# Softmax sums' reciprocals spread over partitions and multiplied onto the product with v

## The chip, the cores and the metric

One core of a Trainium2 chip runs the whole program. The metric is the device time of one execution in microseconds (us), as the median of several runs. The engines are PE (TensorE: matmuls and transposes), ACT (ScalarE), DVE (VectorE), POOL (GpSimd) and SP (SyncE, which here only issues DMAs, in order, from one queue). SBUF is the on-chip memory, PSUM the memory that PE writes its sums to, and DRAM the chip's large memory.

## The reference

Attention with a block mask, then two feed-forward layers. The part that the change touches is the softmax, whose rows are divided by their sum before the product with v.

```
q, k, v: (4, 8, 576, 64)                       # batch, heads, sequence, head size
scores = q @ k.T / sqrt(64), masked where block_i < block_j (blocks of 64)
attn = exp(scores - max)
attn = attn / (sum(attn, axis=-1) + 1e-9)
x = (attn @ v) as (2304, 512)
h = x @ w_in (512 x 2048);   y = (max(h, 0) + log1p(exp(-|h|))) @ w_out (2048 x 512)
h = y @ u1 (512 x 1024);     s = h * softmax(h)
out = ((s - mean) / sqrt(var + 1e-6) * g_ln) @ u2 (1024 x 512)
```

## The kernel before

All work is cut into tasks (`add(engine, model ns, rank, function, dependencies)`). A planner (`Plan.run`) plays the tasks through with model durations, takes on each engine the ready task of lowest rank, and so fixes the order of the instructions of every engine; each engine then works through its list strictly in that order. The rank of a task is its local rank plus the numbers of two tables, `OFF` (by task) and `RANK` (by group).

Float32 values are split into a high and a low part (`..._hi`, `..._lo`, on paper x = hi + lo) so that PE can multiply them in a faster form with three matmuls (hi·hi, hi·lo, lo·hi). The groups are:

- **Piece**: one of 32 pieces of the weights w1 and w2 (512 KB each, 16 of each). `load` brings `raw` by DMA, `signed` (ACT) and `bits0`, `bits1` (DVE) turn it into a float32 `a`, `do_hi` (ACT or DVE) and `do_lo` (DVE) make the two parts of `w`.
- **UnitA**: two heads of one batch, the first 256 positions; 16 units, four to a chunk of 256 tokens (chunks 0 to 3). Tasks: `mm_qk` (PE), `mask`, two `max`, `scale` (DVE), `exp` (ACT, which also adds up the sums `dA`), `den0`, `den1` (DVE: sum + 1e-9, reciprocal), `norm` (DVE: four multiplications of `eA` by its rows' reciprocals), `tr` (PE transposes of `eA`), `copy` (to `psA`, ACT or DVE), `pv` (PE: product with v), `x_hi`, `x_lo` (to `xt`, the input of the first layer). Scores, transposes and product share a PSUM bank named `R`, `r`, `acc` or `hp`.
- **UnitC**: two heads of one batch, the other 320 positions; 16 units, for chunks 4 to 8. The 320 rows are worked on in three parts i = 0, 1, 2, with score matmuls S of 384, 512 and 288 columns; I write S(0), S(1), S(2). Per part: `mm_qk`, `mask`, `max`, `exp` (to `eC`, sums `dC`), `den0`, `den1`, `norm` (five multiplications a unit, ACT or DVE), `split` (16-bit halves to `hl`), `tr` (a DMA transpose back into `eC`, issued by SP), `merge` (DVE, to `ps`). Then `pv` (PE, to `O`), `x_hi`, `x_lo`.
- **Pair**: two of the 16 blocks of w1/w2 for one chunk. `a` (24 matmuls of 256 columns, `hp<-xt,w`), `abs`, `exp`, `ln` (ACT), `stt`, `do_gh`, `do_gl` (DVE), `b` (24 matmuls, `acc<-gh/gl,w`, for chunk 1 `R<-...`). 8 pairs a chunk, 72 in all. The list `SEQ` sets the order of the `a` parts: chunk 0 leads chunk 1 by LAG pairs, and each `a` waits for the one before it in `SEQ`; from chunk 2 on the chunks follow each other. The first `a` of a chunk needs the whole `xt` of that chunk.
- **Tok**: 18 blocks of 128 tokens through the second layer (`h<-...`, then `op<-...`).

The stages overlap: units of chunks 0 and 1 with the conversion of the weights (0 to about 53 us), then the pairs of chunks 0 and 1 with the rest of the conversion, UnitA of chunks 2 and 3, UnitC among the pairs (about 200 to 465 us), the last pairs, and Tok to the end.

Of the kernel before, what the change touches and what calls it, by code (L numbers as in the profile page):

```python
# [24 lines left out]
    "Pair.evac": -5005.0, "Pair.exp": -16485.4, "Pair.ln": -8885.4, "Pair.store": -7128.0, "Pair.stt": 8391.0,
    "Piece.bits0": 1146.4, "Piece.bits0@P0": -7429.7, "Piece.bits1": -9495.3, "Piece.bits1@P0": 8715.1,
    "Piece.do_hi": 9838.9, "Piece.do_hi@P0": 3547.5, "Piece.do_hi_g": 507.8, "Piece.do_lo": 6538.2,
    "Piece.do_lo@P": -11296.2, "Piece.do_lo@P0": -11338.9, "Piece.do_lo_g": 6022.5, "Piece.load": 13705.4,
    "Piece.load@P0": 16755.6, "Piece.signed": 15163.0, "Piece.signed@P0": -783.6, "Tok.a": 1079.7,
    "Tok.aggr": -16861.9, "Tok.bm": 10531.9, "Tok.center": -6983.1, "Tok.exp": 7716.2, "Tok.ln_hi": 9220.6,  # L30
    "Tok.ln_lo": 2618.6, "Tok.load": -16248.9, "Tok.logexp": -10340.8, "Tok.max": -5855.7, "Tok.merge": -13609.8,
    "Tok.mul": -11643.0, "Tok.o_evac": 12110.8, "Tok.small1": 12073.6, "Tok.small2": -5198.1, "Tok.split": -1245.7,
    "Tok.split_hi": 598.2, "Tok.split_lo": -8460.0, "Tok.stats": -9589.2, "Tok.store": 34066.3, "Tok.tr": -8072.5,
# [189 lines left out]
def body(ctx: ExitStack, tc: tile.TileContext, qk, qkA, vP, vA, w1, w2, u1, u2, gln, out):  # L223
# [126 lines left out]
    class UnitC:  # L350
# [96 lines left out]
        def max(self, i):  # L447
            self.m, self.den = self.t([128, 2], "mC", 3), self.t([128, 2], "dC", 3)
            n = 2 if i < 2 else 1
            DVE.tensor_reduce(out=self.m[:, 0:n], in_=self.scores(i), axis=AX.X if i < 2 else AX.XY, op=ALU.max, negate=True)  # L450
            self.stat = getattr(self, "stat", {})
            self.stat[i] = (self.m, self.den, n)

        def exp(self, i, j):
            m, den, _ = self.stat[i]
            e, sc = state["eC"][i][:, j, :], self.scores(i)
# [4 lines left out]
            ACT.activation(e, sc, AF.Exp, bias=m[:, j:j + 1], accum_out=den[:, j:j + 1])  # L461

        def den0(self, i):
            _, den, n = self.stat[i]
            DVE.tensor_scalar_add(den[:, 0:n], den[:, 0:n], 1e-9)

        def den1(self, i):
            _, den, n = self.stat[i]
            DVE.reciprocal(den[:, 0:n], den[:, 0:n])

        def norm(self, i, j, e):
            p, r = state["eC"][i][:, j, 0:WC[i]], self.stat[i][1][:, j:j + 1]
            if e == "ACT":
                ACT.activation(p, p, AF.Copy, scale=r)
            else:
                DVE.tensor_scalar(p, p, r, None, op0=ALU.mult)  # L476
# [601 lines left out]
```

## Time and profile before

| | us |
|---|---|
| median of 3 runs (760.71 to 765.06) | 762.73 |
| the profiled execution's own time | 761.89 |
| its span, first to last instruction | 760.1 |
| PE busy | 736.1 (97%) |
| DVE busy | 592.5 (78%) |
| ACT busy | 442.3 (58%) |

Matmuls are pipelined: a matmul's duration in the trace is longer than the distance to the next one, so runs of equal matmuls are read by the length of the run divided by their count. Line numbers (L606) are those of the kernel before; L232 is the helper that issues every matmul and L238/L240 the helper `copy` on ACT and on DVE.

### The profile page before, as it was taken

The page shows a single profiled execution, that of the slowest core. Times are in us where ns is not written, and L with a number is a line of the kernel's source. Part 1 is how long each engine was busy: PE and PEld are TensorE (multiplying, and loading weights), DVE is VectorE, ACT ScalarE, POOL GpSimd, SP SyncE. Part 2 cuts the span into 40 slices and gives each one's busy share as a digit, 9 for nine tenths or more (in the row PEclk, how much of TensorE's full clock was granted, in tenths as well). Part 3 has the DMA queues.
Part 4 walks back from the last instruction along what each step waited for, and adds up shares of the span by engine and source line. Part 5 has one row for each costly group of instructions (what it writes and reads, how often), then busy time and mean ns, then how long its engine had stood idle before and what let it go on. Part 6 is the DMA issues. An engine that isn't in the chain of part 4 may idle for free.

```text
span 760.1 us, 13785 instructions
## 1 busy us (share of the span) xinstructions
PE 736.1 (97%) x5304; PEld 650.0 (86%) x5304; DVE 592.5 (78%) x1273; ACT 442.3 (58%) x914; POOL 0.7 (0%) x6
## 2 busy tenths in 40 slices
PE   7678999999999999999999999999999999999998
PEld 4568999989988888888888889999998888888887
DVE  6999984476777888788889685656978998898882
ACT  6758774474877777877777772653923433333331
POOL 0000000000000000000000000000000000000000
PEclk9889999999999999999999999999999999999999
DMA  6665720121566556665556644325414554344322
GB/s 214 210 226 184 238 87 22 61 63 45 93 138 129 111 117 178 126 130 136 116 112 129 137 98 106 103 93 190 130 42 97 124 98 101 95 95 84 83 63 77
DMA packets 148002, 88.99 MB, mean 117 GB/s; under 512 B 119648, under 2 KB 131168, under 8 KB 147936
## 3 DMA queue, kind: packets, MB, share of 16 engines
q1 hardware_dynamic: 147936, 88.10, 46.6%
q8 instruction: 42, 0.69, 0.4%
q14 instruction: 24, 0.20, 0.1%
HBM read 49.29 MB, written 9.44 MB: 77 GB/s over the span
## 4 chain that ended last, share of the span: by engine, by line
PE 79%; DMA 8%; DVE 8%; ACT 3%; issue 1%; SPq 0%; ACTq 0%; DVEq 0%
PE hp L232 21%; PE acc L232 19%; PE op L232 13%; PE h L232 13%; DMA eC<-hl 6%; PE S L232 4%; PE R L232 4%; PE O L232 3%; PE r L232 2%; ACT eC L461 1%; DMA raw<-in_w_dram 1%; DVE ps L498 1%; DVE mC L450 1%; PE r L613 1%; DVE t L698 1%
## 5 line engine op out<-in xcount | busy, mean ns | idle before, releaser
L232 PE MATMUL hp<-xt,w 128*128 128x256 f32 x1728 | 219.7, 282 | 3.1 <-DVE t L698 1.9
L232 PEld LDWEIGHTS hp<-xt,w 128*128 128x128 f32 x1728 | 207.5, 190 | 13.8 <-issue 9.7
L232 PE MATMUL acc<-gh,w 128*128 128x256 f32 x768 | 146.1, 283 | 0.6 <-DVE gh L240 0.6
L232 PEld LDWEIGHTS acc<-gh,w 128*128 128x128 f32 x768 | 122.9, 191 | 3.8 <-issue 1.6
L232 PE MATMUL acc<-gl,w 128*128 128x256 f32 x384 | 108.0, 281 | 0.3 <-DVE gl L706 0.3
L232 PE MATMUL h<-u,w 128*128 128x512 f32 x432 | 100.7, 389 | 0.0
L232 PE MATMUL op<-w,w2w 128*128 128x512 f32 (+1 forms) x456 | 100.5, 378 | 0.0
L232 PEld LDWEIGHTS op<-w,w2w 128*128 128x128 f32 x456 | 82.5, 188 | 16.0
L232 PEld LDWEIGHTS h<-u,w 128*128 128x128 f32 x432 | 80.8, 188 | 16.5
L232 PEld LDWEIGHTS acc<-gl,w 128*128 128x128 f32 x384 | 73.1, 190 | 0.7 <-DVE gl L706 0.6
L689 ACT ACTIVATE t<-hp 128x512 f32<-128x512 f32 x72 | 42.7, 594 | 46.9 <-PE hp L232 40.5
L698 DVE SCALAR_TENSOR_TENSOR t<-hp,t 128x512 f32<-128x512 f32 x72 | 49.3, 684 | 18.6 <-ACT t L695 18.3
L498 DVE COPY ps<-eC 128x1536 uint16<-128x1536 uint16 (+2 forms) x48 | 45.8, 954 | 21.2 <-DMA eC<-hl 21.2
L461 ACT ACTIVATE eC<-S,mC 128x384 f32<-128x384 f32 (+2 forms) x80 | 52.0, 650 | 12.8 <-DVE mC L450 9.2
L706 DVE TENSOR_TENSOR gl<-t,gh 128x512 fp32r<-128x512 f32 x72 | 49.5, 687 | 2.1 <-ACT gh L238 1.4
L450 DVE TENSOR_REDUCE mC<-S 128x2 f32<-128x768 f32 (+2 forms) x48 | 46.6, 971 | 3.7 <-PE S L232 3.2
L232 PE MATMUL acc<-gh,w2w 128*128 128x256 f32 x256 | 48.6, 281 | 0.0
L692 ACT ACTIVATE t<-t 128x512 f32<-128x512 f32 x72 | 45.4, 631 | 1.1
L695 ACT ACTIVATE t<-t 128x512 f32<-128x512 f32 x72 | 45.3, 628 | 1.4
L238 ACT ACTIVATE hl<-eC 128x768 uint16<-128x768 uint16 (+2 forms) x46 | 38.7, 847 | 10.1 <-DVE eC L476 9.7
L238 ACT ACTIVATE hl<-e 128x1024 uint16<-128x1024 uint16 x18 | 18.9, 1057 | 39.9 <-DVE e L939 39.8
L232 PEld LDWEIGHTS acc<-gh,w2w 128*128 128x128 f32 x256 | 40.5, 188 | 1.0 <-issue 0.8
(153 smaller groups left out, 1087.5 us busy)
## 6 DMA issues: line engine op xcount, KB each, us to landing
raw<-in_w_dram SPq DMA_DIRECT2D x32, 512.0 KB, 4.4
qkC<-in_qk_dram SPq DMA_DIRECT2D x16, 480.0 KB, 4.6
raw_u<-in_u_dram SPq DMA_DIRECT2D x11, 512.0 KB, 3.5
v<-in_vP_dram SPq DMA_DIRECT2D x16, 320.0 KB, 3.0
x2s<-stg SPq DMA_DIRECT2D x18, 256.0 KB, 2.2
xr<-x2s SPq DMA_DIRECT2D x18, 256.0 KB, 3.3
qkA<-in_qkA_dram SPq DMA_DIRECT2D x16, 256.0 KB, 3.6
out_dram<-ob SPq DMA_DIRECT2D x15, 256.0 KB, 2.0
```

Of the source, the lines that this page charges most:

```text
L232: PE.matmul(out, lhsT, rhs, start=start, stop=stop, skip_group_check=True)
L238: ACT.activation(out, a, AF.Copy)
L450: DVE.tensor_reduce(out=self.m[:, 0:n], in_=self.scores(i), axis=AX.X if i < 2 else AX.XY, op=ALU.max, negate=True)
L461: ACT.activation(e, sc, AF.Exp, bias=m[:, j:j + 1], accum_out=den[:, j:j + 1])
L498: DVE.tensor_copy(dst, src)
L613: PE.transpose(self.banks[j][:, sl], self.e[:, j, sl], ident)
L689: ACT.activation(self.t, self.hp, AF.Abs)
L692: ACT.activation(self.t, self.t, AF.Exp, scale=-1.0)
L695: ACT.activation(self.t, self.t, AF.Ln, bias=1.0)
L698: DVE.scalar_tensor_tensor(out=self.t, in0=self.hp, scalar=0.0, in1=self.t, op0=ALU.max, op1=ALU.add)
L706: DVE.tensor_sub(self.gl, self.t, self.gh)
```

## The change

In UnitC, `den0` and `den1` run once a unit over five columns of sums instead of three times; `den2` turns that tile in 32x32 blocks (DVE) so that the reciprocals of 128 rows lie along four short rows; `rs_store` writes these to DRAM with four DMAs, `rs_load` reads them back with four DMAs, each value broadcast to 64 partitions, and `scale` multiplies the product `O` by them into `xn`, from which `x_hi` and `x_lo` now read. The five `norm` tasks are gone, and `split` follows `exp` directly.

In UnitA the same is done for the first eight units (chunks 0 and 1) with PE: `spread` issues four matmuls of the reciprocals (as a 128x64 operand that repeats one column) with the identity, `copy_r` brings the result to SBUF, `scale_x` multiplies the product by it. The transposes follow `exp` directly. Units 8 to 15 keep `norm`.

LAG goes from 1 to 3, and both tables have new numbers throughout, so that the order of nearly every engine is another one. The core of the diff:

```diff
-    "Pair.a": -539.0, "Pair.abs": 19481.1, "Pair.b": 843.6, "Pair.do_gh": 13285.1, "Pair.do_gl": -5408.9,
+    "Pair.a": 3386.8, "Pair.abs": 21900.6, "Pair.b": 5240.6, "Pair.do_gh": 15092.3, "Pair.do_gl": -3380.6,
...
-    XTB, LAG = 3, 1
+    XTB, LAG = 3, 3
...
+    sums = [dram.tile([5, 128], F32, name=f"sums{n}") for n in range(B * H // 2)]
...
-                t = chain("DVE", r, ((140, partial(self.den0, i)), (140, partial(self.den1, i))), e)
-                n = [add({"ACT": 100 + .833 * w, "DVE": 70 + .55 * w}, None, r, partial(self.norm, i, j), [t]) for j in heads]
...
-                n = [add({"ACT": 100 + .833 * cols, "DVE": 75 + .52 * cols}, None, r, partial(self.split, i, k), n + back) for k in range(2)]
+                n = [add({"ACT": 100 + .833 * cols, "DVE": 75 + .52 * cols}, None, r, partial(self.split, i, k), e + back) for k in range(2)]
...
+            t = chain("DVE", 15, ((70, self.den0), (80, self.den1), (90, self.den2)), list(self.t_exp.values()) + g(p2, "t_rs"))
+            self.t_rs = add("SP", 1680, 15, self.rs_store, [t], 2000.0)
+            self.t_rr = add("SP", 1680, 16, self.rs_load, [self.t_rs] + (p2.t_x if p2 else []), 2000.0)
+            self.t_pv = add("PE", 2272, 24, self.pv, cps + [self.t_v] + g(p1, "t_xn"))
+            self.t_xn = add("DVE", 400, 22, self.scale, [self.t_pv, self.t_rr])
...
+        def den2(self):
+            DVE.transpose(self.dt, self.den)
+
+        def rs_store(self):
+            for n in range(4):
+                SP.dma_start(out=sums[4 * self.b + self.pr][:, 32 * n:32 * n + 32], in_=self.dt[32 * n:32 * n + 5])
+
+        def rs_load(self):
+            self.r, rs = self.t([128, NB], "rC", 2), sums[4 * self.b + self.pr]
+            for j in range(2):
+                to = self.r[64 * j:64 * j + 64]
+                SP.dma_start(out=to[:, 0:256].rearrange("p (i q) -> p i q", i=2), in_=rs[2 * j:2 * j + 2].partition_broadcast(64))
+                SP.dma_start(out=to[:, 256:NB], in_=rs[4, 64 * j:64 * j + 64].partition_broadcast(64))
...
+        def scale(self):
+            self.xn = self.r
+            DVE.tensor_mul(self.xn, state["O"][:, 0:NB], self.r)
...
-            t = chain("DVE", rank, ((72, self.den0), (90, self.den1), (918, self.norm)), [t])
-            self.t_tr = add("PE", 650, rank, self.tr, [t])
...
+            if n < 8:
+                t = chain("DVE", rank, dens, [self.t_exp])
+                self.t_tr = add("PE", 650, rank, self.tr, [self.t_exp])
...
+            if n < 8:
+                t = add("PE", 460, rank, self.spread, [self.t_cp, t])
+                t = add({"ACT": 264, "DVE": 335}, None, rank, self.copy_r, [t])
...
+        def spread(self):
+            self.rr = self.banks[1][:, 0:NA]
+            for i in range(2):
+                for j in range(2):
+                    mm(self.rr[64 * j:64 * j + 64, 128 * i:128 * i + 128], self.den[:, i, j:j + 1].broadcast_to([128, 64]),
+                       ident, i == 0, i == 1)
...
+        def scale_x(self):
+            DVE.tensor_mul(self.r, self.o, self.r)
+            self.o = self.r
```

Three places show how the change moves instructions. First, DVE near its beginning, while it works on the first units (line numbers are those of each kernel; `eA`, `dA`, `mA` are a unit's exponentials, sums and maxima, `hp_114` and the like PSUM tiles). Before:

```order
L598 TENSOR_SCALAR dA<-dA 128x4
L588 TENSOR_SCALAR mA<-mA 128x4
L601 RECIPROCAL dA<-dA 128x4
L606 TENSOR_SCALAR eA_130<-eA_130,dA 128x128 x2
L606 TENSOR_SCALAR eA_130<-eA_130,dA 128x256 x2
L598 TENSOR_SCALAR dA<-dA 128x4
L580 MEMSET hp_114 64x2x64
L580 MEMSET hp_115 64x2x64
L601 RECIPROCAL dA<-dA 128x4
```

With the change, the same place:

```order
L621 TENSOR_SCALAR dA<-dA 128x4
L611 TENSOR_SCALAR mA<-mA 128x4
L624 RECIPROCAL dA<-dA 128x4
L244 COPY psA<-R 128x768
L603 MEMSET hp_130 64x2x64
L603 MEMSET hp_131 64x2x64
L621 TENSOR_SCALAR dA<-dA 128x4
L608 TENSOR_REDUCE mA<-hp_130 128x1
L608 TENSOR_REDUCE mA<-hp_131 128x1
L624 RECIPROCAL dA<-dA 128x4
L244 COPY psA<-r 128x768
```

The four multiplications of the first unit are gone, and in their place stand copies of transposes out of PSUM (`psA`), which wait for PE; before, ACT made the first of these copies.

Second, PE at the end of the first eight units (`hp<-xt,w_f` is the `a` part of a pair with block f of w1; the first rows are transposes and products of units of chunk 1). Before:

```order
L613 MATMUL R<-ident,eA_133 128x128 x6
L232 MATMUL R<-psA,vA 64x256 x2
L232 MATMUL R<-psA,vA 64x128 x2
L613 MATMUL r<-ident,eA_132 128x128 x6
L232 MATMUL r<-psA,vA 64x256 x2
L232 MATMUL r<-psA,vA 64x128 x2
L232 MATMUL hp_115<-xt,w_0_81 128x256 x12
L232 MATMUL hp_115<-xt,w_1_82 128x256 x12
L232 MATMUL hp_114<-xt,w_2_83 128x256 x12
L232 MATMUL hp_114<-xt,w_3_84 128x256 x12
```

With the change, where the last two units of chunk 1 get their scores:

```order
L236 MATMUL r<-psA,vA 64x256 x2
L236 MATMUL r<-psA,vA 64x128 x2
L236 MATMUL r<-ident,dA 64x128 x4
L236 MATMUL R<-qkA 128x128 x2
L236 MATMUL R<-qkA 128x256 x2
L236 MATMUL hp_131<-xt,w_2_99 128x256 x12
L236 MATMUL hp_131<-xt,w_3_100 128x256 x12
L236 MATMUL r<-qkA 128x128 x2
L236 MATMUL r<-qkA 128x256 x2
L643 MATMUL R<-ident,eA_149 128x128 x6
```

Before, `hp_115<-xt,w_0` is the first pair of chunk 1 and only one pair of chunk 0 stands ahead of it. With the change the second pair of chunk 0 (`w_2`, `w_3`) stands ahead of the last transposes of chunk 1, and the first pair of chunk 1 comes behind 120 matmuls of pairs of chunk 0 instead of 48.

Third, SP's queue in the stage of UnitC (transposes of part 0, 1, 2 have 12, 16, 10 blocks). Before, one unit:

```order
L488 DMA_TRANSPOSE eC_2151<-hl_2154 128x12x128
L426 DMA v<-in_vP_dram 128x640
L406 DMA qkC<-in_qk_dram 128x960
L488 DMA_TRANSPOSE eC_2152<-hl_2155 128x16x128
L488 DMA_TRANSPOSE eC_2153<-hl_2156 128x10x128
```

With the change, a unit of even number:

```order
L497 DMA_TRANSPOSE eC_2257<-hl_2260 128x12x128
L433 DMA v<-in_vP_dram 128x640
L497 DMA_TRANSPOSE eC_2258<-hl_2261 128x16x128
L413 DMA qkC<-in_qk_dram 128x960
L478 DMA sums_59<-dT_2252 5x32 x4
L484 DMA rC<-sums_59 64x256
L485 DMA rC<-sums_59 64x64
L484 DMA rC<-sums_59 64x256
L485 DMA rC<-sums_59 64x64
L497 DMA_TRANSPOSE eC_2259<-hl_2262 128x10x128
```

In units of even number the eight new DMAs stand ahead of the transpose of part 2; in those of odd number they stand behind it.

## Rows read from the trace of the kernel before

**Rows 1.** The page's first part: busy time, share, instructions.

```profile
PE 736.1 (97%) x5304; PEld 650.0 (86%) x5304; DVE 592.5 (78%) x1273; ACT 442.3 (58%) x914; POOL 0.7 (0%) x6
```

**Rows 2.** Windows: length, busy time of each engine, granted clock, DMA share, GB/s.

```profile
5.00:53.00 48.00, 36.33 (x225) 26.50 (x223) 44.39 (x137) 33.24 (x100) 0.00 (x0) 0.86 0.65 222
...
60.00:100.00 40.00, 39.19 (x325) 38.76 (x326) 38.23 (x79) 32.12 (x63) 0.00 (x0) 0.96 0.65 209
...
200.00:465.00 265.00, 261.52 (x2131) 227.75 (x2130) 215.18 (x466) 194.82 (x401) 0.00 (x0) 1.00 0.62 129
465.00:757.00 292.00, 291.80 (x1717) 257.61 (x1716) 226.85 (x433) 118.47 (x205) 0.00 (x0) 1.00 0.39 98
...
24.50:31.40 6.90, 4.81 (x22) 4.21 (x24) 6.51 (x23) 5.47 (x17) 0.00 (x0) 0.51 0.67 245
```

**Rows 3.** PE's timeline, 25 to 54 us: start, length, group, idle before.

```profile
26.59 1.69 PE L613 MATMUL R<-ident,eA 128*128 128x128 f32 x6 [4.09 <-DVE eA L606]
...
31.84 0.87 PE L613 MATMUL r<-ident,eA 128*128 128x128 f32 x6
...
47.10 0.87 PE L232 MATMUL R<-psA,vA 128*64 128x256 f32 x8 [0.90 <-ACT psA L238]
...
53.09 1.08 PE L232 MATMUL hp<-xt,w 128*128 128x256 f32 x7 [1.11 <-DVE xt L632]
```

**Rows 4.** The chain that ended last, in order of time: a late pair.

```profile
518.45 2.72 PE hp L232 x24
```

**Rows 5.** DVE's groups from 5 to 53 us: count, busy us, mean ns, idle before.

```profile
L308 DVE SCALAR_TENSOR_TENSOR a<-raw,a 128x512 int32<-128x512 int32 x12 | 8.0, 683 | 0.0
L606 DVE TENSOR_SCALAR eA<-eA,dA 128x128 f32<-128x128 f32 (+1 forms) x32 | 8.0, 313 | 0.0
L318 DVE TENSOR_TENSOR w<-a,w 128x512 fp32r<-128x512 f32 x11 | 7.3, 682 | 0.0
...
L632 DVE TENSOR_TENSOR xt<-R,xt 128x256 fp32r<-128x256 f32 x3 | 1.3, 417 | 0.0
...
L240 DVE COPY psA<-r 128x768 f32<-128x768 f32 x1 | 0.9, 949 | 0.0
...
L698 DVE SCALAR_TENSOR_TENSOR t<-hp,t 128x512 f32<-128x512 f32 x1 | 0.7, 671 | 0.0
L706 DVE TENSOR_TENSOR gl<-t,gh 128x512 fp32r<-128x512 f32 x1 | 0.7, 665 | 0.0
...
L240 DVE CAST xt<-R 128x256 fp32r<-128x256 f32 x1 | 0.4, 412 | 0.0
L240 DVE CAST gh<-t 128x512 fp32r<-128x512 f32 x1 | 0.4, 410 | 0.0
```

**Rows 6.** Groups of the whole span, the normalisations of UnitC.

```profile
L474 ACT ACTIVATE eC<-eC,dC 128x384 f32<-128x384 f32 (+2 forms) x34 | 22.2, 670 | 21.3 <-DVE dC L469 21.1
...
L476 DVE TENSOR_SCALAR eC<-eC,dC 128x512 f32<-128x512 f32 (+2 forms) x46 | 20.5, 459 | 0.7
```

**Rows 7.** Who PE waited for: us in total, times, longest.

```profile
PE S L232 <- ACT eC L461: 3.5, 7, 0.9
```

**Rows 8.** SP's timeline, 249 to 254.4 us.

```profile
249.47 0.33 SPq L406 DMA_DIRECT2D qkC<-in_qk_dram  x1
250.12 4.21 SPq L488 DMA_TRANSPOSE eC<-hl  x1
```

**Rows 9.** DMA issues: KB each and median us to landing; the transposes of L488.

```profile
x2s<-stg SPq DMA_DIRECT2D x18, 256.0 KB, 2.2
...
DMA to landing us min/median/max: 3.4/3.7/6.6
```

**Rows 10.** Groups by form: the steps of part 2 of a UnitC.

```profile
L450 DVE TENSOR_REDUCE mC<-S 128x1 f32<-128x576 f32 x16 | 12.1, 755 | 3.2 <-PE S L232 3.2
...
L461 ACT ACTIVATE eC<-S,mC 128x576 f32<-128x576 f32 x16 | 11.7, 729 | 1.3 <-DVE mC L450 1.3
...
L498 DVE COPY ps<-eC 128x1024 uint16<-128x1024 uint16 x16 | 10.9, 680 | 0.0
```

More of the change, by code (lines that the diff above doesn't have):

```diff
@@ L23 @@
 OFF = {
-    "Pair.a": -539.0, "Pair.abs": 19481.1, "Pair.b": 843.6, "Pair.do_gh": 13285.1, "Pair.do_gl": -5408.9,
[L25 to L33, printed above, removed]
@@ L34 @@
-    "Tok.x_hi": -10387.3, "Tok.x_lo": 929.2, "UnitA.copy": -6891.8, "UnitA.copy@A0": -10849.8,
[12 rows of a table removed]
-    "UnitC.load_v": 4551.1, "UnitC.mask": -2395.7, "UnitC.max": -7859.6, "UnitC.merge": 5530.3, "UnitC.merge4": 330.1,
-    "UnitC.mm_qk": -3300.8, "UnitC.norm": 8858.1, "UnitC.pv": -8537.0, "UnitC.qk_hi": 1098.8, "UnitC.qk_lo": -21328.7,
-    "UnitC.split": 218.0, "UnitC.tr": -12959.4, "UnitC.x_hi": 10326.6, "UnitC.x_lo": -1399.5, "UnitC.xx": 8868.7,
+    "Pair.a": 3386.8, "Pair.abs": 21900.6, "Pair.b": 5240.6, "Pair.do_gh": 15092.3, "Pair.do_gl": -3380.6,
@@ new lines @@
+    "Pair.evac": -4950.5, "Pair.exp": -10309.3, "Pair.ln": 4149.9, "Pair.store": -5244.9, "Pair.stt": 14059.9,
+    "Piece.bits0": 11178.8, "Piece.bits0@P0": -10103.1, "Piece.bits1": -2575.3, "Piece.bits1@P0": 4062.5,
+    "Piece.do_hi": 17753.6, "Piece.do_hi@P0": -3766.5, "Piece.do_hi_g": 4833.8, "Piece.do_lo": -10750.8,
+    "Piece.do_lo@P": 4460.2, "Piece.do_lo@P0": -12688.1, "Piece.do_lo_g": 20393.4, "Piece.load": 21724.5,
+    "Piece.load@P0": 1092.7, "Piece.signed": 8820.7, "Piece.signed@P0": -19749.9, "Tok.a": -9758.0,
@@ new lines @@
+    "Tok.aggr": -21470.1, "Tok.bm": -1073.3, "Tok.center": -6910.1, "Tok.exp": 10676.5, "Tok.ln_hi": 8914.0,
+    "Tok.ln_lo": 7416.6, "Tok.load": -13410.9, "Tok.logexp": -9396.8, "Tok.max": 10445.1, "Tok.merge": -13936.6,
+    "Tok.mul": 2821.1, "Tok.o_evac": 8258.9, "Tok.small1": 8572.0, "Tok.small2": -10072.8, "Tok.split": -2091.8,
+    "Tok.split_hi": -23674.2, "Tok.split_lo": -10254.2, "Tok.stats": 4834.9, "Tok.store": 21152.1, "Tok.tr": -24273.3,
+    "Tok.x_hi": -22912.3, "Tok.x_lo": -5993.3, "UnitA.copy": -5166.2, "UnitA.copy@A0": -18405.5,
[14 rows of a table added]
@@ L50 @@
+    "UnitC.load_qk": -730.6, "UnitC.load_v": -942.4, "UnitC.mask": 5069.0, "UnitC.max": -13097.1,
+    "UnitC.merge": -1660.1, "UnitC.merge4": 18467.6, "UnitC.mm_qk": 5854.1, "UnitC.norm": -3475.3,
+    "UnitC.pv": -7142.9, "UnitC.qk_hi": -2723.1, "UnitC.qk_lo": -3998.8, "UnitC.rs_load": -1874.7,
+    "UnitC.rs_store": -1204.5, "UnitC.scale": 3388.1, "UnitC.split": -5309.1, "UnitC.tr": 4654.6,
+    "UnitC.x_hi": 6403.1, "UnitC.x_lo": -14603.0, "UnitC.xx": 4346.6,
 }
 RANK = {
[3 rows of a table removed]
-    "Tok": (20529.5, 1935.38),
[3 rows of a table added]
@@ L395, in plan @@
                 args = (c, off, done, w)
-                ta = add({"ACT": act_ns(w) + 40, "DVE": dve_ns(w)}, None, 22, partial(self.x_hi, *args), [self.t_pv, ta] + xfree(c))
+                ta = add({"ACT": act_ns(w) + 40, "DVE": dve_ns(w)}, None, 22, partial(self.x_hi, *args), [self.t_xn, ta] + xfree(c))
                 tb = add("DVE", dve_ns(w), 22, partial(self.x_lo, *args), [ta, tb])
@@ L447, in max @@
         def max(self, i):
[L448 to L452, printed above, removed]
+            if i == 0:
+                self.m, (self.den, self.dt) = self.t([128, 5], "mC", 2), state["dC"][self.pr % 2]
+            DVE.tensor_reduce(out=self.m[:, i:4:2] if i < 2 else self.m[:, 4:5], in_=self.scores(i), axis=AX.X if i < 2 else AX.XY, op=ALU.max, negate=True)
         def exp(self, i, j):
-            m, den, _ = self.stat[i]
-            e, sc = state["eC"][i][:, j, :], self.scores(i)
+            e, sc, c = state["eC"][i][:, j, :], self.scores(i), slice(*((2 * j + i, 2 * j + i + 1) if i < 2 else (4, 5)))
             if i < 2:
@@ L460, in exp, with den0, den1 @@
                 e = e[:, 0:WC[2]].rearrange("p (a b) -> p a b", a=2)
[L461 to L476, printed above, removed]
+            ACT.activation(e, sc, AF.Exp, bias=self.m[:, c], accum_out=self.den[:, c])
+        def den0(self):
+            DVE.tensor_scalar_add(self.den[:, 0:5], self.den[:, 0:5], 1e-9)
+        def den1(self):
+            DVE.reciprocal(self.den[:, 0:5], self.den[:, 0:5])
+        def den2(self):
[9 more added lines that the diff above has]
+                SP.dma_start(out=to[:, 256:NB], in_=rs[4, 64 * j:64 * j + 64].partition_broadcast(64))
         def split(self, i, n, e):
@@ L510, in pv @@
                     mm(o[64 * j:64 * j + 64, q0:NB], self.v[:kk, j, t, :], rhs, t == 0, t == 4)
+        def scale(self):
+            self.xn = self.r
+            DVE.tensor_mul(self.xn, state["O"][:, 0:NB], self.r)
         def x_hi(self, c, off, done, w, e):
-            copy(e, xt_of(c)[:, 0, self.pr, off:off + w], state["O"][:, done:done + w])
+            copy(e, xt_of(c)[:, 0, self.pr, off:off + w], self.xn[:, done:done + w])
         def x_lo(self, c, off, done, w):
             x, pr = xt[c], self.pr
-            DVE.tensor_sub(x[:, 1, pr, off:off + w], state["O"][:, done:done + w], x[:, 0, pr, off:off + w])
+            DVE.tensor_sub(x[:, 1, pr, off:off + w], self.xn[:, done:done + w], x[:, 0, pr, off:off + w])
     class UnitA:
@@ L625, in pv, with copy_r @@
                     mm(self.o[64 * j:64 * j + 64, 128 * t:], self.v[:, j, t, :], self.ps[:, j, 256 * t:256 + 128 * t], t == 0, t == 1)
+        def copy_r(self, e):
+            self.r = self.e[:, 0, 0:NA]
+            copy(e, self.r, self.rr)
+        def scale_x(self):
+            DVE.tensor_mul(self.r, self.o, self.r)
+            self.o = self.r
         def x_hi(self, e):
@@ L751, in open_b @@
         state["O"] = q.tile([128, 512], F32, name="O")
+        state["dC"] = [[state["pat"].tile([128, 32], F32, name=f"d{x}{i}") for x in "CT"] for i in range(2)]
+        for d, _ in state["dC"]:
+            DVE.memset(d, 1.0)
         state["eC"] = [state["pat"].tile([128, 2 if i < 2 else 1, w], F32, name=f"eC{i}") for i, w in enumerate((WC[0], WC[1], WC[2] + 64))]
```

12 lines of the change are left out of this document (9 added, 3 removed), and 32 rows, old and new, of tables (OFF, RANK).

## The prediction

> **What bounds the kernel now.** The page's first part comes first: PE is busy for 97% of the span and no other engine for more than 78% [rows 1]. What a change elsewhere is worth must therefore come from the places where PE is not busy, and the windows find them [rows 2]. From 465 to 757 us PE lacks 0.2 of 292 us: nothing is to be had there. From 200 to 465, the stage of UnitC, it lacks 3.5 of 265. From 60 to 100 it lacks 0.8 of 40. From 5 to 53 it lacks 11.7 of 48, and there the reader is to see DVE with 44.4 busy microseconds of 48: DVE is the bound of the start, and PE from about 53 us on.
>
> PE's timeline shows what ends the start [rows 3]. At 53.09 us it goes on with `hp<-xt,w` after 1.11 us of waiting for `x_lo` (L632) of the eighth unit. That is the first pair of chunk 1, which LAG = 1 puts behind a single pair of chunk 0. From there PE has work without a break, so the end of the program is that moment plus PE's remaining work. The start is changed by two things only: when the eighth unit is done, and how much pair work PE has behind it by then.
>
> **The start, part by part.**
>
> *Pair work moved ahead.* The order of PE has 120 matmuls of pairs ahead of the first pair of chunk 1, against 48. A run of 24 takes 2.72 us [rows 4], so one takes 113 ns, and 72 of them are 8.2 us that no longer follow that moment.
>
> *DVE's work up to the eighth unit.* Off goes `norm`, 32 instructions of 313 ns, 10.0 us by their own durations [rows 5]. On come eight `scale_x`, which read PSUM and SBUF as `x_lo` does at 417 ns, 3.3 us; three more `psA` copies that the planner gives to DVE, at 949 ns, 2.8 us; four copies of 256 columns at 412 ns (two `copy_r`, two more `x_hi`), 1.6 us; `stt`, `gh` and `gl` of a second pair, 671 + 410 + 665 ns, 1.7 us; and one more piece's `bits1` and `do_lo`, 683 + 682 ns, 1.4 us, about paid for by two casts of weights and small things that go. The sum on is 10.8, off 10.0 and 0.8: nothing. What `norm` frees on DVE is spent before the eighth unit is done, most of it on what brings the pairs ahead.
>
> *New waits on DVE.* Of the 48 us DVE is idle for 3.6 [rows 2]. With the change the `psA` copies of the first units stand early on DVE and wait there for PE's transposes, and `scale_x` waits for `pv`, `spread` and `copy_r`; behind them on DVE stand the maxima of the next units and the first `bits`. A group of six transposes takes 1.69 us at the low clock and 0.87 at the high one [rows 3]. The bounds are nothing (each copy finds its transposes done) and one slow group for each of the first four units, 6.8 us. Walking down the order I find about 1 us at the first copy, half of that at the second, and about 1 us each at the third copy and the first `scale_x`: I take the middle, 3.4 us.
>
> *`spread` on PE.* No row shows it. The nearest is `pv`: eight matmul records with 768 columns in 0.87 us [rows 3]; `spread` has as many records with 512 columns, so 0.6 us, and twice that at the low clock. Eight are 4.6 us (9.3). They lie ahead of the moment, where PE waits anyway: 120 matmuls (13.6 us), three groups of about 0.87 us for each of eight units (20.9) and 4.6 make 39.1 us, between about 10 and 56 us. That leaves some 7 us for the low clock. If this cover were gone, the eight would cost their 4.6 us. I take 0, with 0 to 4.6 as bounds.
>
> So the start gives 8.2 - 3.4 = 4.8 us. Its bounds are 8.2 (no new wait) and -3.2, a loss (6.8 of waits and an uncovered `spread`, 8.2 - 6.8 - 4.6).
>
> **The stage of UnitC.** Gone are 34 multiplications on ACT (22.2 us) and 46 on DVE (20.5 us) [rows 6]; but ACT and DVE are busy for 195 and 215 of these 265 us [rows 2], and only PE's waits count: 3.5 us, which PE waits for `exp` before it writes S again [rows 7]. In the new order S(2) stands farther behind S(1) in every second unit, so half of this should go: -1.7 us, bounds 0 and -3.5.
>
> Against it stand eight new DMAs a unit on SP. In units of odd number they are behind the transpose of part 2. In units of even number that transpose waits behind them: from S(2) on the path is `max` 755 ns, `exp` 729 [rows 10], four issues at 0.33 us (1.3), landing 2.2 as for `x2s`, four issues again (1.3), the transpose 3.7 us to landing (6.6 at most) [rows 8, 9], `merge` 680 ns [rows 10]: 10.7 us, at most 13.6. Three small DVE operations and two DMA landings of a kind that no row shows are in neither figure beyond this. The new order gives 108 pair matmuls between S(2) and `pv` in these units, 12.2 us, and 72 in the others, 8.2 us, where the same path without the eight DMAs takes 5.9 to 8.8. So `pv` waits between nothing and about 1.4 us in eight even units, and 0.6 in the odd ones: 0 to 16 us. Most transposes land near the median, so I take a tenth of a microsecond a unit, 0.7 in the even units together. The path's largest unknown is how soon the transpose starts behind other transfers: behind `qkC` its issue held the queue for 4.21 us [rows 8].
>
> The Trainium skill's page "DMA: Bandwidth & Descriptors" (section "Anatomy of one DMA") puts about 2 us of fixed cost on each DMA, most of it the receipt of the last write, and calls DRAM the slowest target. This speaks against a round trip through DRAM: by that figure the store and the load together would take an estimated 4 us where I count 2.2 once and let the loads land under the transpose, and an even unit's path would come to 12.5 us with a median transpose (10.7 - 2.2 + 4.0), 0.3 over its room of 12.2, or 2.4 us in eight units. The 2.2 us of the trace agrees for the store; what the load's landing costs no row shows.
>
> So the stage gives 1.7 - 0.7 = 1.0 us. The table also starts the second layer's first block later; PE's room there is 0.2 us of idle time, and I price this at 0, with up to 3 us against it.
>
> **The sum.** 4.8 + 1.0 = 5.8 us off the profiled execution's 761.9 gives 756.1. The median of the runs is 0.8 above that execution, so 756.9: I say 757.
>
> **The rivals.**
>
> *The queue decides (slower).* The transposes of part 2 land late behind the new DMAs, at their 6.6 us instead of 3.7, so that `pv` waits in every unit. For it speaks that a transpose behind a plain transfer held SP for 4.21 us, and that the distance from S(2) to `pv` shrinks to 72 matmuls in every second unit. Against it speaks that DVE already waits for transposes and PE does not. Price: 16 us at most, I take 12 and the start's gain kept: 762.7 - 4.8 + 12, about 770. It decides as soon as an even unit's path exceeds 12.2 us by 0.6 (0.6 x 8 = 4.8).
>
> *The start gives nothing.* The new waits on DVE reach 6.8 us, or pieces of the weights come too late once PE uses twelve of them before chunk 1: then 8.2 - 6.8 = 1.4 us, and 761. For it speaks that DVE's sum of work does not fall at all.
>
> *The start gives all.* The granted clock was 0.51 from 24.5 to 31.4 us [rows 2], the 1.2 GHz level, after PE had idled for 4.09 us [rows 3]. If a PE with more to do stays at 2.4 GHz, the transposes take 0.87 instead of 1.69 us, the new waits vanish, and the start gives 8.2 us: 762.7 - 8.2 - 1.0 = 753.5. The page "TensorE: Matmul & The Clock Gate" of the Trainium skill (section "What's actually happening") says that the clock is granted by recent activity of the array, which is this rival's rule; this trace agrees in that the low stretch follows an idle one.
>
> **How the numbers follow.** Half a percent (3.8 us) is about what a measurement of this kernel can tell from no change; the bounds are 758.9 and 766.5. The likeliest case (start pays, UnitC neutral) has 0.50, with its own range of 752 to 760, and lies below 758.9 for 0.42 of it. The queue has 0.20, of which 0.02 stays within half a percent. The start giving nothing has 0.20: 0.17 within, 0.03 slower. The start giving all has 0.10, all of it faster. Together: faster 0.52, the same 0.27, slower 0.21. The range is 750 to 769: below lies only the last rival with every wait of UnitC gone, above it the upper half of the first.
>
> **What would show it.** Right: the first pair of chunk 1 on PE at about 56 to 57 us, five runs of 24 pair matmuls ahead of it, DVE's idle time up to there near 7 us; no `pv` of UnitC that waits for DVE `merge` by more than a few tenths; and PE's waits for `exp` in this stage at half. Wrong: PE's `O<-ps` waiting for `merge` in every unit, or transposes of part 2 that land more than 6 us after the loads; or the first pair of chunk 1 at 60 us. If PE's idle time after 465 us exceeds 1 us, the later start of the second layer was not free.

## The result, and the profile after

The median is 751.27 us (750.71 to 751.63, 4 runs) against 762.67 for the kernel before: a ratio of 0.9848 (95% interval 0.9819 to 0.9877), 11.4 us less where 5.7 were forecast. The range, 750 to 769, holds it; the size is off by a factor of two. The same kernel run again (e18) gave 751.94 (750.75 to 756.42; 0.9872, 0.9836 to 0.9909).

Behind a median stand, in parentheses, the lowest and highest run and the ratio to the kernel before with its 95% interval. Each ratio is to runs of the kernel before taken beside that experiment, whose medians went from 760.84 to 763.22. A few executions that took far longer than all the others of their kernel are left out of these figures. Every kernel has one trace, of a single execution.

The page's first part after the change and windows (length, busy time of PE, PEld, DVE, ACT, POOL, granted clock, DMA share, GB/s):

```profile
PE 728.7 (97%) x5368; PEld 648.0 (86%) x5368; DVE 580.7 (78%) x1185; ACT 421.6 (56%) x876; POOL 0.7 (0%) x6
```

```profile
5.00:57.00 52.00, 43.14 (x369) 36.06 (x368) 47.27 (x126) 38.55 (x112) 0.00 (x0) 0.97 0.68 222
...
61.00:66.00 5.00, 5.00 (x44) 5.00 (x44) 4.96 (x13) 4.26 (x9) 0.00 (x0) 1.00 0.78 243
...
200.00:465.00 265.00, 261.00 (x2156) 228.30 (x2155) 206.37 (x401) 179.98 (x370) 0.00 (x0) 1.00 0.64 139
465.00:746.00 281.00, 280.91 (x1629) 248.02 (x1627) 225.40 (x427) 114.60 (x197) 0.00 (x0) 1.00 0.40 100
```

In [rows 2] the start had a clock of 0.86 up to 53 us; here it is 0.97 up to 57. Between 200 and 465 us PE idles about as long as before (4.0 us against 3.5), though the window holds other work. PE's timeline at the end of the first eight units:

```profile
27.33 1.38 PE L643 MATMUL R<-ident,eA 128*128 128x128 f32 x6 [4.70 <-ACT eA L617]
28.36 2.83 PE L236 MATMUL hp<-xt,w 128*128 128x256 f32 x12
...
50.46 0.61 PE L236 MATMUL r<-ident,dA 128*64 128x128 f32 x8
51.00 3.10 PE L236 MATMUL hp<-xt,w 128*128 128x256 f32 x24
...
55.34 2.99 PE L236 MATMUL hp<-xt,w 128*128 128x256 f32 x24
58.26 0.93 PE L236 MATMUL r<-qkA 64*128 64x128 f32 x8
60.14 3.10 PE L236 MATMUL hp<-xt,w 128*128 128x256 f32 x24 [0.95 <-DVE t L736]
```

The first pair of chunk 1 starts at 55.34, against 53.09 [rows 3], with five runs of 24 pair matmuls ahead of it. `spread` takes 0.61 us, as estimated. Who PE waited for from 75 to 480 us (total, times, longest):

```profile
PE O L236 <- DVE ps L507: 3.3, 4, 2.0
PE S L236 <- ACT eC L465: 0.7, 2, 0.3
```

The waits of [rows 7] are nearly gone, and `O` now waits for `merge`, four times and at most 2.0 us. The kernel before shows no wait of `O` in this window.

To place the gain I add up PE's matmuls in the order of time, each kind at its undisturbed interval (113 ns for one of a pair, `spread` left out), and read when the same amount of work was done:

| PE work done (us) | before, at us | after, at us | difference |
|---|---|---|---|
| 40 | 75.97 | 68.54 | -7.4 |
| 160 | 204.24 | 196.48 | -7.8 |
| 300 | 362.18 | 349.30 | -12.9 |
| 400 | 471.03 | 460.68 | -10.4 |
| all | 756.80 | 745.91 | -10.9 |

So between these two executions the start gave 7.4 us (4.8 forecast), the stage of UnitC, from 160 to 400 of work, 2.6 (1.0 forecast): it gains 5.1 and gives 2.5 back. The Tok stage gave 0.5 (0). "Of the start" and "of the stage" below are read at 40 and between 160 and 400 of this work, against this trace of the kernel before.

The start of the kernel before is not the same in every execution. Experiment e5 below changes UnitC alone, so its start is that of the kernel before, and there 40 us of work are done 2.2 us earlier. The first pair of chunk 1 starts at the same moment in both (53.16 and 53.09); the difference comes behind it. The kernel before:

```profile
60.81 4.42 PE L232 MATMUL hp<-xt,w 128*128 128x256 f32 x24 [1.93 <-DVE t L698]
```

```profile
56.31 0.43 DVE L305 TENSOR_SCALAR a<-a 128x512 int32<-128x512 int32 x1 [1.00 <-ACT a L302]
```

```profile
61.00:66.00 5.00, 5.00 (x31) 5.00 (x31) 4.96 (x12) 2.88 (x6) 0.00 (x0) 0.66 0.89 279
```

The same place in e5:

```profile
53.16 5.09 PE L232 MATMUL hp<-xt,w 128*128 128x256 f32 x41 [1.11 <-DVE xt L628]
58.19 0.93 PE L232 MATMUL r<-qkA 64*128 64x128 f32 x8
59.70 3.09 PE L232 MATMUL hp<-xt,w 128*128 128x256 f32 x24 [0.59 <-DVE t L694]
```

```profile
61.00:66.00 5.00, 5.00 (x45) 5.00 (x44) 4.60 (x11) 4.41 (x9) 0.00 (x0) 1.00 0.84 276
```

In the kernel before DVE had waited 1.00 us for ACT's `a`, a piece of the weights; its `t` came 1.1 us later, PE waited 1.93 us instead of 0.59, and the granted clock was then 0.66, partly at 1.2 GHz, instead of 1.00. So a difference of some 2 us of the start against this one trace shows no cause by itself; against e5 the start of the changed kernel gave 5.2 us.

### The profile page after: what moved, and what is told of

Its sections match the earlier page's. It is cut to its first block, busy times and chain, and to the rows that moved or that the text cites. A ratio compares the mean times of both kernels' runs of the same rounds, so it can differ in the third digit from the quotient of the medians.

```text
span 749.2 us, 13919 instructions
## 1 busy us (share of the span) xinstructions
PE 728.7 (97%) x5368; PEld 648.0 (86%) x5368; DVE 580.7 (78%) x1185; ACT 421.6 (56%) x876; POOL 0.7 (0%) x6
## 4 chain that ended last, share of the span: by engine, by line
PE 71%; DVE 11%; DMA 11%; ACT 3%; SPq 3%; issue 2%; DVEq 0%; ACTq 0%
PE hp L236 17%; PE acc L236 16%; PE op L236 13%; PE h L236 13%; DMA raw<-in_w_dram 4%; PE O L236 3%; PE S L236 3%; DMA eC<-hl 3%; PE R L236 2%; DMA sums<-dT 2%; DVE ps L507 1%; DMA rC<-sums 1%; DVE a L313 1%; SPq L484 1%; PE r L236 1%
## 5 line engine op out<-in xcount | busy, mean ns | idle before, releaser
L236 PE MATMUL hp<-xt,w 128*128 128x256 f32 x1728 | 216.2, 281 | 0.9 <-DVE t L736 0.9
L236 PEld LDWEIGHTS acc<-gh,w 128*128 128x128 f32 x768 | 121.1, 188 | 3.9 <-issue 3.4
L727 ACT ACTIVATE t<-hp 128x512 f32<-128x512 f32 x72 | 42.7, 594 | 62.8 <-PE hp L236 53.2
L242 ACT ACTIVATE hl<-eC 128x1024 uint16<-128x1024 uint16 (+2 forms) x45 | 38.7, 860 | 0.6
```

Of the source, the lines that this page charges most:

```text
L236: PE.matmul(out, lhsT, rhs, start=start, stop=stop, skip_group_check=True)
L242: ACT.activation(out, a, AF.Copy)
L727: ACT.activation(self.t, self.hp, AF.Abs)
```

## Experiments: the start

The prediction's theory: 72 pair matmuls moved, less new waits on DVE, with the low clock covered by other work. Its rival: the clock is a part of the gain.

**e8: LAG = 1 in the changed kernel; e13: LAG = 2.**

```diff
-    XTB, LAG = 3, 3
+    XTB, LAG = 3, 1
```

> The changed kernel with LAG = 1 again, all else kept. Prediction's step (72 pair matmuls moved, 8.2 us, against 3 to 5 us of DVE work that brings them): 755 to 759. With the clock as part of the gain (LAG 3 keeps PE busy enough to stay at 2.4 GHz between 38 and 66 us): half-clock stretches come back there as in the kernel before, and the start loses 6 us or more: 757 to 759.

> The changed kernel with LAG = 2, all else kept. By the moved matmuls alone (half of 72 times 113 ns): 4 us slower, 755. If the clock and the waits behind it are a part of it, half-clock stretches return between 40 and 70 us and it is 6 to 9 us slower: 757 to 760.

e8 measured 763.42 (761.48 to 765.1), e13 759.24 (757.17 to 760.56): the changed kernel without its LAG has lost its whole gain. PE's timeline of e8 and two windows:

```profile
53.75 1.65 PE L236 MATMUL r<-qkA 64*128 64x128 f32 x8 [2.25 <-DVE eA L662]
55.34 8.09 PE L236 MATMUL hp<-xt,w 128*128 128x256 f32 x48
65.86 1.14 PE L643 MATMUL r<-ident,eA 128*128 128x128 f32 x6 [2.43 <-DVE eA L629]
67.08 4.57 PE L236 MATMUL hp<-xt,w 128*128 128x256 f32 x24
```

```profile
53.00:57.00 4.00, 3.25 (x16) 2.60 (x17) 3.97 (x10) 1.96 (x4) 0.00 (x0) 0.55 0.84 242
57.00:63.00 6.00, 6.00 (x40) 6.00 (x40) 5.52 (x14) 2.39 (x7) 0.00 (x0) 0.73 0.88 285
```

The first pair of chunk 1 starts at 55.34 with LAG = 1 and with LAG = 3: the moved pairs delay the eighth unit by nothing. But at 40 of work e8 is 13.9 us behind the changed kernel, not 8.2. 48 pair matmuls take 8.1 us where they would take 5.4, and 24 take 4.6 instead of 2.7: 4.5 of the other 5.7 us are in these two rows. Both follow waits of PE, and the granted clock is 0.70 from 55.3 to 63.4 us and 0.63 from 67 to 71.6, so partly at 1.2 GHz. For e13, 36 matmuls are 4.1 us; the start lost 5.4 and the median 8.

**e4: LAG = 3 alone in the kernel before.**

> The kernel before with LAG = 3 alone: its tables and both normalisations stay. Prediction's step: 72 pair matmuls move ahead of the first pair of chunk 1 (8.2 us), against 3 to 5 us of DVE work for two more pairs: 757 to 760. Rival: without DVE time freed by the missing multiplications that work delays the eighth unit as much as it gains, or more: 762 to 766.

758.52 (755.87 to 762.73; ratio 0.9957, 0.9934 to 0.9979). The start gains 6.1 us with every `norm` in place (3.9 against that of e5): that DVE pays for the pairs with the time of `norm` is refuted. The median gains 2.8, so later stages, planned with the old tables, give some of it back.

**e3: the kernel before without `norm` in the first eight units; e12: the changed kernel with the old UnitA.** In e3 `norm` returns at once for n < 8; in e12 the class is that of the kernel before.

> The kernel before without the 32 DVE multiplications of the first eight units (their output stays undivided), order kept. If DVE is the bound of the start, its 10 us of work are worth most of their length there: the first pair of chunk 1 at 45 to 49 us instead of 53.1, and 755 to 759. If the chain of the units, the loads or the casts of the weights set the start, under 2 us: 761.

> The changed kernel with the first eight units as before (norm on DVE, nothing spread by PE), planned with the new tables; LAG = 3 and UnitC as changed. If norm's 10 us of DVE time pay for the pairs that LAG = 3 brings ahead: the first pair of chunk 1 is 4 to 8 us later and the median 755 to 759. If the start is bound by other things (LAG = 3 alone gained 6 us of the start in the kernel before): 751 to 753.

e3: 761.02 (757.29 to 764.44; 0.9989, 0.9964 to 1.0014); taking 10 us of work off DVE brings the first pair of chunk 1 to 51.58, 1.5 us earlier. Its traced execution, 757.38, is one of its fastest and gains 4.4 us of the start, 2.2 of which e5 gains too. e12: 753.08 (749.49 to 755.35; 0.9871, 0.9840 to 0.9901), 1.8 above the changed kernel, with intervals that overlap. By its trace the new way of the first eight units is worth 1 us of the start. DVE is busy, but not the only bound.

**e1, e15, e17: products that nothing reads, in PE's idle time of the kernel before; e2, e16: the same in the changed kernel.**

```diff
+    def fill(n):
+        for i in range(n):
+            mm(acc[:, 0, 0:128], ident, ident, True, True)
...
         def tr(self):
+            state["tr_n"] = state.get("tr_n", 0) + 1
+            fill({5: 15}.get(state["tr_n"], 0))
...
         def mm_qk(self):
+            state["mq_n"] = state.get("mq_n", 0) + 1
+            fill({8: 8}.get(state["mq_n"], 0))
```

> The kernel before, with 30 extra 128x128 products of the identity on PE ahead of the fifth unit's transposes (where PE idled 4.1 us) and 16 ahead of the eighth unit's scores (where it idled 2.0 us); nothing reads them. Prediction's own step (DVE is the bound of the start, the clock only stretches work that is covered): within 1 us of before, about 762.7. Clock theory: the two stretches at half the clock (24.5 to 31.4 and 38.2 to 45.0 us) go; in them 12 pair matmuls took 2.8 us where they take 1.4, and 24 took 5.6 where they take 2.7, so about 4 us less: 758.5.

> The kernel before with half as many extra products (15 and 8, so that they fit into PE's idle time). The half-clock stretches of 24 to 45 us shorten or go. If the clock before 53 us is covered (DVE sets the moment of the eighth unit): the first pair of chunk 1 within 1 us of 53.1 and the median within 2 us of the kernel before. If not: 3 to 4 us faster.

> The kernel before with 15 and 8 extra products, a second time: 757. If the gain is the clock's: no half-clock stretch between 24 and 66 us, and PE at the same work some 4 us earlier than the kernel before by 70 us. If it came from the stage of UnitC by other landing times: the start within 1 us, and PE's waits of S for exp under 1 us.

The products of e1 overran the gap: each is two matmul records, so 30 took 6.96 us; e1 measured 767.77 (0.8% slower: 1.0081, 1.0049 to 1.0113). Its start is 2.8 us ahead of the kernel before (0.6 ahead of e5); all of that and more goes in the stage of UnitC, where `S` waits 8.8 us for `exp` instead of 3.5. Why, with the same order, stays open.

With half as many, e15 measured 756.89 (0.9935, 0.9911 to 0.9958) and e17, the same program again, 755.99 (0.9924, 0.9899 to 0.9949). PE's timeline of e17:

```profile
21.53 3.62 PE L232 MATMUL acc<-ident 128*128 128x128 f32 x30
25.79 1.13 PE L619 MATMUL R<-ident,eA 128*128 128x128 f32 x6 [0.65 <-DVE eA L611]
26.68 1.66 PE L232 MATMUL hp<-xt,w 128*128 128x256 f32 x12
...
51.89 4.93 PE L232 MATMUL hp<-xt,w 128*128 128x256 f32 x41 [1.10 <-DVE xt L638]
...
58.55 3.09 PE L232 MATMUL hp<-xt,w 128*128 128x256 f32 x24 [0.87 <-DVE t L704]
```

And its windows from 24.5 to 31.4 us, where [rows 2] has a clock of 0.51, and from 61 to 66:

```profile
24.50:31.40 6.90, 5.80 (x48) 4.93 (x48) 6.27 (x21) 4.46 (x13) 0.00 (x0) 1.00 0.64 215
```

```profile
61.00:66.00 5.00, 5.00 (x45) 5.00 (x44) 4.73 (x10) 5.00 (x16) 0.00 (x0) 1.00 0.54 181
```

Work that nobody uses makes the kernel before some 5 us faster. The start gains 3.4. Of these, 1.2 us come at the moment of the eighth unit (51.89 against 53.09, and 53.16 in e5): the low clock ahead of it was not wholly covered. The Trainium skill's page "TensorE: Matmul & The Clock Gate" (section "What's actually happening") has activity release the throttle; the trace agrees, since from 24.5 to 31.4 us the clock is 1.00 with these products and 0.51 without (0.56 in e5). The other 2.2 us, behind that moment, are not shown to be the products' work: e5 has them without a single one, and runs the same 45 matmuls from 61 to 66 us. Another 2.2 us come in the stage of UnitC, where `S` waits 1.1 us; they are of the kind that e1 lost, and open.

> The changed kernel with 34 such extra products ahead of the fifth unit's transposes, where PE idled 4.7 us. Clock theory: the one stretch at half the clock that is left (27 to 31 us) goes; 12 pair matmuls in it took 2.8 us where they take 1.4, the transposes 1.4 where they take 0.9: up to 2 us less, 749.3. Prediction's own step (DVE is the bound): no change, 751.3.

> The changed kernel with 17 extra products ahead of the fifth unit's transposes, half of those before, so that they fit into the 4.7 us of idle time. If the half-clock stretch from 27 to 31 us that is left costs time: 1 to 2 us faster, 749.5 to 750.3. If it is covered: 751.3.

e2: 751.93 (751.51 to 753.55; 0.9871, 0.9844 to 0.9898); e16: 754.24 (749.57 to 758.86; 0.9903, 0.9869 to 0.9937). The granted clock is 1.00 from 27 to 31 us in both, and nothing is gained: in the changed kernel the one half-clock stretch that is left is covered. e16 is the less steady: in its traced execution, 756.36, `O` waits 7.5 us for `merge`.

## Experiments: the stage of UnitC

**e5: the kernel before without UnitC's multiplications; e9: the changed kernel with 80 put back; e11: the changed kernel with the old UnitC.** e5 returns at once from `norm`; e9:

```diff
             ACT.activation(e, sc, AF.Exp, bias=self.m[:, c], accum_out=self.den[:, c])
+            e = state["eC"][i][:, j, 0:WC[i]]
+            if (i + j + self.pr) % 2:
+                ACT.activation(e, e, AF.Copy, scale=1.0)
+            else:
+                DVE.tensor_scalar(e, e, 1.0, None, op0=ALU.mult)
```

> The kernel before without the 80 multiplications of UnitC (the product stays undivided for chunks 4 to 8), order and reciprocals kept. If the multiplications stood on the path from exp to the transposes, and so to the next unit's exp and S: PE's waits of S for exp (3.5 us) fall under 1 us and the median by 3 to 4, to about 758. If only the new order of PE (S(2) farther behind S(1)) takes these waits away, as the prediction has it: they stay at 3 to 4 us, about 761.

> The changed kernel with 80 multiplications of UnitC's exponentials (by 1.0) put back behind each exp, 40 on ACT and 40 on DVE, the order of everything else kept. If what UnitC gained (2.6 us in the profiles) comes from the new order: within 1.5 us of the changed kernel, 751 to 753. If it comes from the time that ACT and DVE no longer spend on multiplying: PE's waits of S for exp are back (3.5 us and more) and the median is 754 to 757.

> The changed kernel with UnitC as before (multiplications of the exponentials, no trip through DRAM), planned with the new tables; LAG = 3 and the first eight units as changed. The start should keep its 7.5 us: first pair of chunk 1 at 55 to 56 us. If UnitC is worth 2.6 us: 753 to 755; if the new table alone carries it and the trip only costs: 747 to 750.

e5: 761.73 (0.9997, 0.9970 to 1.0024), and `S` still waits 2.7 us for `exp`: in the old order 42.7 us of ACT and DVE work are worth nothing. e9: 762.99 (760.58 to 764.39): in the new order the same work costs 12 us. The waits of PE, and one of DVE's, in e9:

```profile
PE O L236 <- DVE ps L512: 5.8, 6, 1.9
PE S L236 <- ACT eC L465: 3.3, 8, 1.2
PE S L236 <- DVE qkl L429: 1.3, 3, 0.6
```

```profile
DVE eC L470 <- ACT eC L465: 13.9, 23, 2.0
```

DVE waits 13.9 us at the multiplications put back, which a planned order would place better, so 12 is an upper bound. e11 is planned with them: 761.78 (0.9992, 0.9974 to 1.0010). Its start is that of the changed kernel within 0.5 us; then its stage loses 9.1 us against it, with `O` waiting 4.5 and `S` 3.7. So neither the new tables nor the absence of the multiplications gains by itself: the new order gains only where `split` follows `exp` directly. The tables were made for the changed kernel, so e8 and e11 also measure how ill they fit another one: each loses the whole gain, and the two losses add up to about twice it. How the old UnitC would do with LAG = 3 and tables made for it stays open.

**e6: no trip through DRAM; e7: the trip on POOL's queue; e10: the trip behind the transpose of part 2.** In e6 the multiplier is a tile of ones; in e7 `SP.dma_start` in the two functions becomes `POOL.dma_start`; e10 moves both functions on SP:

```diff
+            if t.key in ("UnitC.rs_store", "UnitC.rs_load") and id(unit) not in seen:
+                late.setdefault(id(unit), []).append(t)
+                continue
             self.emit(t)
+            if t.key == "UnitC.tr" and args[0] == 2:
+                seen.add(id(unit))
+                for x in late.pop(id(unit), []):
+                    self.emit(x)
```

> The changed kernel with the eight new DMAs of a UnitC left out (the multiplier is a tile of ones written by POOL, so chunks 4 to 8 stay undivided), order kept. If the new DMAs on SP delay the transposes: PE's waits of O for merge (3.3 us in the profile of the changed kernel) go, 748. If these waits come from the transposes themselves: they stay, 751.

> The changed kernel with the eight new DMAs of a UnitC issued by POOL, which does nothing else in this stage, instead of SP; same data, same order on the other engines. If it is SP's queue that makes the transposes of part 2 late: O's waits go and about 3 us with them, 748. If it is the landing of the DMAs or their share of the DMA engines: 751. If issue by POOL is slow enough that the scale waits for its loads: over 753.

> The changed kernel with the eight DMAs of a UnitC moved behind the transpose of part 2 on SP in every unit, all else in the same order. If the place of the DMAs ahead of the transpose is what costs (O waits for merge, 3.3 us; leaving the trip out gave 4.4): 747 to 749. If the trip costs the same wherever it stands, because the scale then waits for its loads and DVE with it: 751 to 753.

e6: 746.88 (744.38 to 748.25): the trip costs 4.4 us, 4.9 of the stage in the profiles; no wait of `O` is left. e10: 749.54 (748.64 to 751.27; 0.9828, 0.9799 to 0.9856), the fastest here that still divides by the sums, 1.7 below the changed kernel. The intervals overlap, so the size is uncertain; that the waits of `O` go, the trace shows. PE's waits in e10, and DVE's for the loads:

```profile
PE S L250 <- ACT eC L479: 1.4, 3, 0.7
PE r L657 <- DVE eA L643: 0.5, 1, 0.5
PE S L250 <- DVE qkl L443: 0.3, 1, 0.3
```

```profile
DVE rC L537 <- DMA rC<-sums: 15.1, 8, 2.8
```

`O` no longer waits; DVE now waits 15.1 us for the loads (9.0 in the changed kernel), and of that PE feels little. e7: 763.75 (758.86 to 765.84), its stage 10.7 us longer: issued by POOL, the DMAs leave DVE's `scale` waiting 33.4 us, and PE waits for what stands behind it on DVE.

The profile shows the trip at its worst unit. SP's timeline of the changed kernel, then PE's and DVE's at the end of it:

```profile
364.55 1.30 SPq L478 DMA_DIRECT2D sums<-dT  x4
368.65 0.46 SPq L484 DMA_DIRECT2D rC<-sums  x1
369.16 0.60 SPq L485 DMA_DIRECT2D rC<-sums  x1
369.80 0.60 SPq L484 DMA_DIRECT2D rC<-sums  x1
370.44 0.59 SPq L485 DMA_DIRECT2D rC<-sums  x1
371.08 7.89 SPq L497 DMA_TRANSPOSE eC<-hl  x3
```

```profile
358.43 0.43 PE L236 MATMUL S<-qkh 128*128 128x288 f32 x2
...
376.22 2.16 PE L236 MATMUL O<-ps,v 128*64 128x320 f32 x16 [1.96 <-DVE ps L507]
```

```profile
362.27 0.19 ACT L465 ACTIVATION_READ_ACCUMULATOR eC<-S,mC 128x1 f32 x1
```

```profile
360.84 0.75 DVE L457 TENSOR_REDUCE mC<-S 128x1 f32<-128x576 f32 x1
...
375.47 0.69 DVE L507 COPY ps<-eC 128x1024 uint16<-128x1024 uint16 x1 [4.12 <-DMA eC<-hl]
```

From S(2) to `O` it is 17.8 us, where the prediction had 10.7, at most 13.6; `O` waits 1.96 us. `max` begins 2.4 us after S(2), behind other work of DVE; the stores begin 2.1 us after `exp`; the first load waits 2.8 us for them to land; four loads hold the queue 2.4 us (1.3 estimated); the transpose has landed 4.4 us after its issue began (3.7).

**e14: e10 with LAG = 4.**

> The changed kernel with the eight DMAs behind the transpose of part 2 (749.5) and LAG = 4. By the moved matmuls (36 to 48 more ahead of the first pair of chunk 1, 4 to 5 us) where PE still idles about 7 us in the first 57: 745 to 747. If the units wait for DVE, which has a third and fourth pair to finish first: 749 to 752.

753.65 (751.75 to 756.29), 4.1 slower than e10. Its start loses 5.9 us on e10: PE stands 4.1 us at the `b` part of a pair, waiting for DVE's `gh`. LAG = 3 is the best of the four tried (1 to 3 in the changed kernel, 3 and 4 in e10).

**e18: the changed kernel again**, 751.94 (above); in its traced execution `O` waits 3.2 us for `merge`. One of its six runs took 756.42, but no trace shows where.

> The changed kernel itself once more, for its spread: 751.3. If its waits of O for the transposes of part 2 vary from execution to execution (16 us was the bound): runs up to 757.

## Why the prediction was right in its direction and too small

That the change is faster had been given a chance of 0.52, so the direction says little for the reasoning. The forecast of 5.8 us missed 2.6 us in the start, 1.6 in the stage of UnitC, 0.5 in the Tok stage and 0.4 between the first two, in the two traces. Two steps failed:

- **The failed step of UnitC: "only PE's waits count", at most the 3.5 us that the profile names, half of it taken, and the trip at 0.7.** Without the trip the stage gains 7.5 us (e6 against the kernel before), more than twice that bound; the trip costs 4.4 (e6 against the changed kernel). The two misses have opposite signs, so that their net, 2.6 against 1.0, came near by luck. Part of the first lies in what an idle time is: a matmul of a pair lasts 281 ns in the trace and the next one starts 113 ns after it, so a wait of PE shorter than the difference does not show as idle. Counted from start to start, the matmuls just ahead of `S` run 7.6 us over their undisturbed interval in this stage of the kernel before and 3.7 in the changed one.
- **The failed step of the start: "from there PE has work without a break", which priced the moved pairs by their own length and all low clock at nothing.** In the changed kernel LAG alone moves the same 72 matmuls and is worth 13.9 us of the start (e8), not 8.2; 4.5 of the difference are pair matmuls at a low clock behind waits. In the kernel before PE also breaks off behind the moment: 1.93 us for `t`, then 31 matmuls from 61 to 66 us where the changed kernel runs 44. How much of this the change itself cured stays open, since e5 lacks the slow stretch without any change of the start.

Term by term:

- **The pairs moved ahead (8.2 us)** held as their own length: with LAG = 1 (e8) the first pair of chunk 1 starts at the same 55.34 us.
- **The new waits on DVE (3.4 us)** were mis-sized by a third: that pair starts 2.25 us later than before. Other executions with the start of the changed kernel have it at 54.48 (e10) to 56.39 (e6), so the size is uncertain by about 1 us. The changed kernel does not wait there any more: the matmuls of a pair run up to 55.34 without idle time. DVE idles 4.7 us up to 57 us where about 7 were forecast.
- **The low clock (0)**: a rival held it with 0.10, as a cure of DVE's waits. Ahead of the moment it costs the kernel before 1.2 us (e17). Of the 7.4 us of the start, 8.2 - 2.25 are the pairs less the waits; the other 1.5 lie behind the first pair of chunk 1. That rival's 753.5 is the nearest of the four times, but the waits on DVE that it wanted gone are there.
- **"What `norm` frees on DVE is spent before the eighth unit is done, most of it on what brings the pairs ahead"** is refuted as the price of the pairs by e4 and e12: LAG = 3 gains 6.1 us of the start (3.9 against e5) with `norm` in place.
- **`spread` at nothing** is not contradicted: 0.61 us each, ahead of the moment; no run leaves it out alone.
- **`S` waits for `exp` (-1.7 us)**: they fall from 3.5 to 0.7, and e5 shows that the multiplications' absence alone does not do it.
- **`pv` waits for the trip (+0.7 us)**: the path took 17.8 us in its worst unit against a room of 12.2. The prediction's own sign, no wait for `merge` beyond a few tenths, failed: there are four, of up to 2.0 us. The Trainium skill's page "DMA: Bandwidth & Descriptors" (section "Anatomy of one DMA") was nearer with about 2 us for each of the two DMAs, though it describes DMAs that POOL issues: on SP the stores alone kept the loads waiting 2.8 us, and on POOL (e7) stores took 2.8 and loads 3.7 us to land. The rival of the queue was right on the place (without the trip, and with it behind the transpose, no wait of `O` is left) and wrong on the size.
- **The Tok stage at nothing** held for its idle time, 0.1 of 281 us after 465; the 0.5 us that it gave are not explained.

## What to carry to other kernels

Where the busiest engine still idles early, price its low clock as well as its gaps: in e8 a wait was paid again in the matmuls behind it, and filling the start with useful work (here pairs of an earlier chunk) gave more than the work's length. Before a difference of 2 us between two traces is put down to a cause, compare two executions of the same program: here the start of the kernel before differed by 2.2 us from one to another. Taking work off engines that are not the bound gave nothing in the old order; putting it back into the new one cost 9 (e11) to 12 us (e9), an upper bound. So such a change is judged together with the order that it allows. A small DMA round trip in a queue that also feeds the critical path is priced by landing times and issue times on that queue, and put behind what the path waits for.

## What the runs showed of the hardware

Idle PE was filled with 15 and 8 identity products that nothing reads, and the kernel before became 0.65% and 0.76% faster in two runs (e15, e17). With 30 and 16 it became 0.8% slower (e1). A wait of PE for `t` of 1.93 us in the kernel before was followed by a granted clock of 0.66 from 61 to 66 us; waits of 0.59 (e5) and 0.87 us (e17) at the same place were followed by 1.00. The same eight DMAs a unit cost 4.4 us on SP's queue and about 17 on POOL's (763.75 against 746.88 without them): there the issue of four stores took 2.1 to 3.0 us in the units from 199 to 260 us, their landing 2.8 and that of the loads 3.7 (medians). The runs of the kernel before beside the experiments spread from 756.5 to 768.2 us, those of the changed kernel from 750.7 to 756.4.
